# A fused attention kernel on one core: the second half of the first q on ScalarE, a K eviction in halves, and two half banks of the tail waited for one by one

## The chip, the cores and the metric

The kernel runs on one core of a Trainium2 chip. The metric is the device time of one execution in microseconds (us), taken as the median of several runs; less is better. The engines are named as in the profile: PE (TensorE: matmuls; PEld are its weight loads), DVE (VectorE), ACT (ScalarE), POOL (GpSimd) and SP (SyncE, which only issues DMAs here). ACTq and SPq are the DMA issues of ACT and SP.

## The reference

Two attention blocks read the same x (2048 tokens of 640), each with its own weights and 32 heads of 20: A is full softmax attention, B a sliding window of 8 keys, 2 apart. A gate of one number per token mixes them.

```python
    x = A_x
    g = _sigmoid((x * gate_w).sum(-1, keepdims=True))
    a = _A_ref(x, A_wqkv, A_wo)        # softmax(q k^T * scale) v, all 2048 keys, then @ wo
    b = _B_ref(x, B_wqkv, B_wo)        # the same over 8 keys at distances 0, 2, .. 14, then @ wo
    return g * a + (1 - g) * b
```

All inputs are bf16, and so is the output (2048 x 640).

## The kernel before

**Tiling.** The heads are taken four at a time ("quads", 8 of them), 32 partitions to a head, and the queries in chunks of 512, so there are 32 groups of (chunk, quad). A group has 64 units (16 blocks of 128 keys x 4 heads). A tile is two or three units: PE writes the scores of each into one PSUM bank of 512 columns (L1731), ACT takes the exponential of all of them in one instruction (L1756), and four units at a time PE multiplies them by v into the bank `obank` (L1801). Some units go to DVE instead of ACT, which makes powers of two by integer arithmetic (L1745, L905). Between the tiles PE, DVE and POOL do all the other work: projections of q, k and v, all of block B, and the output projections of earlier chunks (L632 is the line of their matmuls).

**What sets the order.** A planner (`_Sched`, and generators with priorities) runs at build time. It keeps a clock for each engine, an estimated duration for each task and, per buffer key, the last writer and the readers since. From the keys it derives the semaphore waits: a task waits for what last wrote the keys that it reads, and for the readers and the writer of those that it writes. `accum` adds to a key that another task has begun. What comes out is one fixed list of instructions for each engine. At the end of the start (from L1545 on) the planner's clocks and free times are overwritten by constants, so that what it plans after that follows from those constants.

**The start.** x is loaded, transposed by PE and copied to `xT`; the keys of the first quad are projected in four blocks of 512. The first three are evicted to `kT` by ACT (`k_out`, L1444), each behind a DVE instruction that finds the largest absolute value (L1437). The fourth is projected in two halves of 256 (L1497) into two banks of `score1`; DVE takes the maximum of each half (L1514), and ACT evicts both in one instruction (L1525). The first q is projected in two halves too, half 0 into `obank`, half 1 into the third bank of `score0`. A bound on the scores is subtracted inside the matmul: |q| of half 0 comes from ACT (L1517), of half 1 from DVE (L1522); the largest |k| (L1518) goes into the matrix `KM` (L1520); and PE adds KM x |q| to each half of q (L1531). Then DVE scales the two halves, adds an offset and writes them to `qT` as bf16 (L1535, twice). The first score tile (L1731) reads both halves. Behind L1535 DVE has the first v eviction (L1458), three instructions for constants (L554 to L557) and further v evictions (L833).

**The tail.** The last 512 tokens are four blocks of 128. Their output projection is nearly complete before the last group of heads is; `tail()` adds the last heads' part, with the matmuls at L1212. The columns 512 to 640 of all blocks lie in one bank ("strips", `score1`). The columns 0 to 512 of blocks 2 and 3 lie in two banks kept for them (`side0` and the third bank of `score0`, found in `tail_bank`), those of blocks 0 and 1 in the first two banks of `score0` ("halves"). DVE adds the earlier part to the strips (L1234), ACT evicts blocks 2 and 3 (L1240, twice), and DVE adds and evicts blocks 0 and 1 (L1243, twice). Then each block's 128 rows are stored by a DMA (L1248): blocks 2 and 3 issued by ACT, blocks 0 and 1 by SP. At the end SP waits for all DMAs, one semaphore after the other. The two halves share the buffer key `("score", 0)`, so both L1243 wait for whatever wrote that key last.

Of the kernel before, what the change touches and what calls it, by code (L numbers as in the profile page):

```python
# [10 lines left out]
ALU = mybir.AluOpType  # L11
ACTF = mybir.ActivationFunctionType
# [35 lines left out]
OCT = STEP * SCALE / LN2  # L48
# [324 lines left out]
def _ap(t, off, dims):  # L373

    row = 1
    for n in t.shape[1:]:
        row *= n
    return bass.AP(tensor=t, offset=off, ap=[[row, P]] + [list(d) for d in dims])


def _build(ctx, nc, A_x, A_wqkv, A_wo, B_wqkv, B_wo, gate_w, out):
# [3 lines left out]
    sch = _Sched(nc, ctx)  # L385
    T = sch.task
# [4 lines left out]
    score = [ps(1536, "score0"), ps(1536, "score1")]  # L391
# [4 lines left out]
    side = [t_[:, o_:o_ + 512] for t_, o_ in BANKS]  # L396
# [15 lines left out]
    kT = sb([P, NQ, S], BF16, "kT")  # L412
# [4 lines left out]
    qT = [sb([P, 512], BF16, "qT%d" % i) for i in range(NQF)] + [woBp[:, i, 0:512] for i in (2, 3)]  # L417
# [15 lines left out]
    offs = sb([P, 1], FP32, "offs")  # L433
# [7 lines left out]
    kmx4 = sb([P, 5], FP32, "kmx4")  # L441
# [5 lines left out]
    onesrow = sb([P, 1], FP32, "onesrow")  # L447
# [43 lines left out]
    dvc = lambda n, mode=1: 0.064 + n * 1.0417e-3 / mode  # L491
    actc = lambda n: 0.095 + n * 0.81e-3 if n > 512 else 0.0635 + n * 0.8334e-3
# [5 lines left out]
    def x_load(tcc, dur):  # L498
# [12 lines left out]
      writes=["WvA"], dma=True)  # L511
    T("sp", 12.0, lambda e: e.dma_start(_ap(kvw, WK_OFF, [[D, CN], [1, D]]), wA_v[:, :, D:2 * D]),
      writes=["WkA"], dma=True)
# [11 lines left out]
      reads=["rB"], writes=["ident"])  # L525
# [12 lines left out]
    for j in range(4):  # L538
        T("dve", 0.07, lambda e, j=j: e.memset(onesrow[32 * j:32 * j + 1, :], 1.0), writes=["onesrow"])
        T("dve", 0.1, lambda e, j=j: e.memset(KMmask[32 * j:32 * j + 32, 32 * j:32 * j + 1], -1.0078125),  # L540
          writes=["KMmask"])
    T("dve", 0.06, lambda e: e.tensor_copy(ones2[:, :], _ap(onesrow, 0, [[0, 2]])), reads=["onesrow"], writes=["ones2"])
    for i in range(NQF):
        T("pool", 0.4, lambda e, i=i: e.memset(qT[i][:, :].bitcast(FP32), 0.0), writes=[("qTz", i)])
    T("dve", 0.06, lambda e: e.tensor_scalar(offs[:, :], onesrow[:, :], STEP * TOP, None, op0=ALU.mult),
      reads=["onesrow"], writes=["offs"])
# [174 lines left out]
    qkeys = {}  # L721
# [410 lines left out]
    pre = lambda i: (dst2[:, 0:1024], qabs2[:, 0:1024], stage[:, 2048:3072])[i].bitcast(FP32)  # L1132
    tail_bank = {}

    def paired(of, blk):
        at = lambda j: blk * P + 2 * (j % 64) + j // 64
        return lambda j: of(slice(at(j), at(j) + 63, 2))
# [3 lines left out]
    def fold_mms(o, blk, qs, c0, c1, b_too, fs=range(CN)):  # L1141
        tok = slice(blk * P, (blk + 1) * P)
        if not b_too:
            return [(o, paired(lambda c: oN[1][:, c], blk), woA_l[:, c0:c1])]
        mms = [(o, oB[:, f, tok], woBp[:, f, c0:c1]) for f in range(CN)] if fs[0] == 0 else []
        wl = [woA_d[:, f, c0:c1] for f in range(CN - 1)] + [woA_z[:, c0:c1]]
        return mms + [(o, paired(lambda c, f=f: oTd[:, (QCN - 1) % 2, f, c], blk), wl[f]) for f in fs]
# [53 lines left out]
    def tail():  # L1201
        tout = [_ap(stage, 3 * 1024 + blk * D, [[1, D]]) for blk in range(4)]
        tcol = lambda blk, c0, c1: _ap(stage, 3 * 1024 + blk * D + c0, [[1, c1 - c0]])
        q = [NQ - 1]
        rd = ["oN1"] + WL

        def mm(key, lst, accum, rd=rd):
            def fn(e):
                seen = set()
                for o, l, r in lst:  # L1210
                    for j in range(0, P, 32):
                        ins = e.matmul(o[j:j + 32, :], l(j), r, start=not accum and o.offset // 512 not in seen, stop=True, skip_group_check=True)  # L1212
                    seen.add(o.offset // 512)
                return ins
            T("pe", sum(0.215 if o.shape[-1] > 128 else 0.06 for o, _, _ in lst), fn, reads=rd, mode="col",
              **({"accum": [key]} if accum else {"writes": [key]}))


        b3 = score[1]
        late = range(FE, CN)  # L1220
        rl = [("oTd", (QCN - 1) % 2, k) for k in range(NQ)] + ["woA_d"] + WQ
        strip = lambda blk: b3[:, blk * P:(blk + 1) * P]
        half = lambda blk: score[0][:, blk * 512:(blk + 1) * 512]
        first = lambda o, *a: [(o_, lambda j, l=l: l(slice(j, j + 32)) if not callable(l) else l(j), r) for o_, l, r in fold_mms(o, *a, True, late)]
        mm(("score", 1), [m_ for blk in range(4) for m_ in first(strip(blk), blk, q, 512, D)], False, rl)
        mm(("score", 0), [m_ for blk in range(2) for m_ in first(half(blk), blk, q, 0, 512)], False, rl)
        run_until(("norm", NG - 1))
        mm(("score", 1), [fold_mms(strip(blk), blk, q, 512, D, False)[0] for blk in range(4)], True)
        for blk in (2, 3):
            b = tail_bank[blk]  # L1230
            mm(("side", b), fold_mms(side[b][:, :], blk, q, 0, 512, False), True)
        for blk in range(2):
            mm(("score", 0), fold_mms(half(blk), blk, q, 0, 512, False), True)
        T("dve", dvc(512), lambda e: e.tensor_tensor(  # L1234
            _ap(stage, 3 * 1024 + 512, [[D, 4], [1, P]]), _ap(b3, 0, [[P, 4], [1, P]]),
            stage[:, 2048:3072].bitcast(FP32).rearrange("p (b c) -> p b c", c=P), ALU.add),
          reads=[("score", 1), ("pre", 2)], writes=["tout_r"])
        for blk in (2, 3):
            b = tail_bank[blk]
            T("act", actc(512), lambda e, b=b, blk=blk: e.activation(tcol(blk, 0, 512), side[b][:, :], ACTF.Copy),  # L1240
              reads=[("side", b)], writes=[("tout", blk)])
        for blk in range(2):
            T("dve", dvc(512), lambda e, blk=blk: e.tensor_tensor(  # L1243
                tcol(blk, 0, 512), score[0][:, blk * 512:(blk + 1) * 512], pre(blk), ALU.add),
              reads=[("score", 0), ("pre", blk)], writes=[("tout", blk)])
        for blk in (2, 3, 0, 1):
            row = (QCN - 1) * 512 + blk * P
            T("act" if blk > 1 else "sp", 2.0, lambda e, blk=blk, row=row: e.dma_start(out_v[row:row + P, :], tout[blk]),  # L1248
              reads=[("tout", blk), "tout_r"], writes=[("out", row)], dma=True)
# [131 lines left out]
    def run_until(flag, first=None):  # L1381
        n = 0
        while not done.get(flag):
            if not any(step(ent, 1e9, True) for ent in sorted(gens, key=lambda x: x[0] != first)):
                raise RuntimeError("stuck on %r: %r" % (flag, [e[3] for e in gens]))
            n += 1
# [114 lines left out]
    hcols = lambda h: slice(256 * h, 256 * h + 256)  # L1501
    k3 = lambda h: score[1][:, 512 * h:512 * h + 256]
    q0 = [obank[:, 0:256], side[1][:, 0:256]]
    q0k = ["obank", ("side", 1)]
    for h in range(2):
        T("pe", 0.55, half_proj(k3(h), lambda c: kvw[:, WKP_OFF + c * P:WKP_OFF + c * P + P], 1536 + 256 * h),
          reads=[("WkP", 0)] + XT(3), writes=[("K3", h), ("score", 1)])
    for h in range(2):
# [3 lines left out]
      reads=[("kmx4", i) for i in range(3)], writes=[("kmx", 0)])  # L1512
    for h in range(2):
        T("dve", dvc(256), lambda e, h=h: e.tensor_reduce(  # L1514
            kmx4[:, 3 + h:4 + h], k3(h), AX.X, ALU.max, apply_absolute_value=True),
          reads=[("K3", h)], writes=[("kmx4", 3 + h)])
    T("act", actc(256), lambda e: e.activation(qabs[0][:, 0:256], q0[0], ACTF.Abs), reads=[("Q0", 0)], writes=[("qabs", 0)])  # L1517
    T("dve", 0.1, lambda e: e.tensor_scalar(kmx[:, 0:1], kmx[:, 0:1], kmx4[:, 3:4], kmx4[:, 4:5], op0=ALU.max, op1=ALU.max),  # L1518
      reads=[("kmx", 0), ("kmx4", 3), ("kmx4", 4)], writes=[("kmx", 0)])
    T("dve", 0.2, lambda e: e.tensor_scalar(KM[0], KMmask, kmx[:, 0:1], None, op0=ALU.mult),  # L1520
      reads=[("kmx", 0), "KMmask"], writes=[("KM", 0)])
    T("dve", dvc(256), lambda e: e.tensor_scalar(  # L1522
        qabs[0][:, 256:512].bitcast(U16), q0[1].bitcast(U16)[:, 1:512:2], 0x7FFF, None, op0=ALU.bitwise_and),
      reads=[("Q0", 1)], writes=[("qabsh", 1)])
    t = T("act", actc(512), lambda e: e.activation(kT[:, 0, 1536:2048].rearrange("p (h c) -> p h c", c=256),  # L1525
                                               _ap(score[1], 0, [[512, 2], [1, 256]]), ACTF.Identity, bias=onesrow[:, 0:1]),
          reads=[("K3", 0), ("K3", 1), ("score", 1), "onesrow", ("kmx4", 3), ("kmx4", 4)], writes=[("kT", 0, 3)])
    bank_free[2] = t.end + LAT["act"]
    qah = [("qabs", 0), ("qabsh", 1)]
    for h in range(2):  # L1530
        T("pe", 0.11, lambda e, h=h: e.matmul(q0[h], KM[0], qabs[0][:, hcols(h)], start=False, stop=True, skip_group_check=True),  # L1531
          reads=[("KM", 0), qah[h]], accum=[("Q0", h), q0k[h]])
    v_first()
    for h in range(2):
        t = T("dve", dvc(256), lambda e, h=h: e.tensor_scalar(  # L1535
            qT[0][:, hcols(h)], q0[h], OCT, offs[:, 0:1], op0=ALU.mult, op1=ALU.add),
              reads=[("Q0", h), q0k[h], "offs", ("qTz", 0)], writes=[("qTh", h)])
        if h == 0:
            obank_first = t.end + LAT["dve"]
    bank_free[1] = t.end + LAT["dve"]  # L1540
# [1 line left out]
    v_out()  # L1542
    bank_free[0] = t.end + LAT["dve"] + 0.5
    done[("k", 0)] = done[("q", 0)] = True
    for key in qkeys[0]:  # L1545
        sch.bufs[key][0].end = 18.0655808
    sch.bufs["kT", 0, 3][0].end = 16.4994312
    sch.avail.update(pe=17.6032304, dve=18.2962528, act=16.4994312)
    bank_free[:] = [18.6485808, 16.6514312, 16.6514312]
# [359 lines left out]
    while pvg < NG:  # L1909
# [53 lines left out]
        elif pvg < NG:  # L1963
            run_side(sch.avail["pe"] + 1.0)
    run_until("prefold")
    tail()

    sch.emit()
# [28 lines left out]
```

## Time and profile before

| | |
|---|---|
| median of 3 runs | 790.83 us (790.8 to 791.33) |
| the profiled execution | 791.24 us, of which the span is 789.4 us |
| ACT busy | 769.0 us (97%), 732 instructions |
| PE busy | 752.3 us (95%), 12556 matmuls |
| DVE busy | 721.5 us (91%), 1282 instructions |
| POOL busy | 123.9 us (16%), 230 instructions |
| moved by DMA | 36.16 MB, 46 GB/s over the span |

A time in the timeline counts from the start of the span. A row gives the start, the time from the first to the end of the last instruction of the row, the engine, the line, the operation, the tiles written and read with their shapes, how many instructions it merges, and in brackets how long the engine had been idle and what released it. [...] A matmul's end is modelled.

### The profile page before, as it was taken

The numbers are of one execution on the slowest core, as the hardware profiler recorded it, in microseconds if no ns is written. First come the engines' busy times: TensorE is split into PE (matmuls) and PEld (weight loads), VectorE is DVE, ScalarE is ACT, GpSimd is POOL, SyncE is SP. The second block draws the span as 40 slices with busy tenths as digits, with TensorE's granted clock in tenths as the row PEclk, the third lists the DMA queues.
The fourth block names the chain that finished last, engine by engine and source line by source line (L and its number), as shares of the span: only waits on it lengthen the run. The fifth ranks groups of instructions, "written<-read, shape, count | busy, mean of one in ns | idle before, by whom it ended". The sixth has DMA issues, their size and how long they took to land.

```text
span 789.4 us, 29584 instructions
## 1 busy us (share of the span) xinstructions
PE 752.3 (95%) x12556; PEld 290.6 (37%) x12556; DVE 721.5 (91%) x1282; ACT 769.0 (97%) x732; POOL 123.9 (16%) x230
## 2 busy tenths in 40 slices
PE   8999999999999999999999999999999999999997
PEld 5423333232233334333334433434443433344323
DVE  7798888999999989999988999998999999898894
ACT  4999999999999999999999999999999999999996
POOL 4011202111112011111111101111111111111210
PEclk9999999999999999999999999999999999999999
DMA  7241121010021123130111312012113013100311
GB/s 227 62 109 25 40 44 33 14 24 18 8 71 30 41 42 73 24 72 16 23 40 42 76 41 58 14 41 71 25 31 71 26 24 71 46 7 7 74 31 40
DMA packets 62663, 36.16 MB, mean 46 GB/s; under 512 B 26884, under 2 KB 61972, under 8 KB 62532
## 3 DMA queue, kind: packets, MB, share of 16 engines
q1 hardware_dynamic: 62244, 33.94, 17.9%
q8 instruction: 100, 1.64, 0.9%
q10 hardware_dynamic: 288, 0.33, 0.1%
q14 instruction: 31, 0.25, 0.1%
HBM read 12.85 MB, written 3.54 MB: 21 GB/s over the span
## 4 chain that ended last, share of the span: by engine, by line
PE 43%; ACT 26%; DVE 17%; issue 11%; SPq 2%; DMA 1%; POOL 0%; DVEq 0%; ACTq 0%
ACT ebuf L1756 25%; PE score L1731 13%; PE obank L1801 12%; PE side L632 12%; DVE uD L1745 6%; DVE eD L905 4%; PE score L632 2%; DVE kvw L1092 1%; SPq L975 1%; DVE qkvB L967 1%; DMA oTd<-in_A_x_dram 1%; PE obank L1822 1%; PE score L1822 1%; PE side L1003 1%; DVE kvw L993 1%
## 5 line engine op out<-in xcount | busy, mean ns | idle before, releaser
L1756 ACT ACTIVATE ebuf<-score 128x1024 bf16<-128x1024 f32 (+1 forms) x699 | 757.0, 1266 | 4.4 <-PE score L1731 3.7
L1745 DVE TENSOR_SCALAR uD<-score 128x512 int16<-128x512 f32 x392 | 260.2, 680 | 14.7 <-PE score L1731 13.3
L1731 PE MATMUL score<-qT,kT 32*128 32x512 bf16 x1856 | 253.8, 384 | 17.7 <-ACT ebuf L1756 13.6
L905 DVE TENSOR_SCALAR eD<-uD 128x2048 int16<-128x2048 int16 x294 | 195.0, 687 | 4.5 <-PE obank L1801 3.4
L1801 PE MATMUL obank<-ebuf,vA 128*21 128x512 bf16 x1656 | 153.5, 385 | 1.7 <-DVE oTt L865 0.6
L1731 PEld LDWEIGHTS score<-qT,kT 32*128 32x128 bf16 x1856 | 63.0, 91 | 211.6 <-ACT ebuf L1756 147.4
L925 POOL TENSOR_TENSOR vS<-vA,vw 128x252 bf16<-128x252 bf16 x98 | 59.9, 613 | 388.5 <-DVE eD L905 252.8
L1801 PE MATMUL obank<-eD,vS 128*21 128x512 bf16 x1176 | 103.5, 379 | 0.0
L632 PE MATMUL side<-xT,wBs 128*32 128x256 bf16 x2400 | 93.6, 280 | 2.2 <-DVE oB L1125 0.7
L632 PEld LDWEIGHTS side<-xT,wBs 128*32 128x32 bf16 x2400 | 68.1, 141 | 27.9 <-issue 14.5
L1801 PEld LDWEIGHTS obank<-ebuf,vA 128*21 128x21 bf16 x1656 | 36.0, 89 | 83.0 <-issue 56.4
L1092 DVE TENSOR_TENSOR kvw<-kvw,eB 128x2048 bf16<-128x2048 bf16 x40 | 48.1, 1214 | 0.2 <-DMA kvw<-qkvB 0.2
L993 DVE TENSOR_TENSOR kvw<-qkvB 128x2048 bf16<-128x2048 bf16 x40 | 48.0, 1215 | 0.1
L882 POOL TENSOR_TENSOR oN<-oTt,rcp 128x256 bf16<-128x256 f32 x62 | 38.8, 625 | 58.0 <-DVE eD L905 39.5
L967 DVE CAST qkvB<-side 128x512 bf16<-128x512 f32 (+1 forms) x72 | 42.0, 593 | 4.5 <-PE side L632 4.3
L873 POOL TENSOR_TENSOR rcp<-rcp,gA 128x16 f32<-128x16 f32 x31 | 9.1, 292 | 192.0 <-DVE eD L905 90.9
L1801 PE MATMUL obank<-uD,vA 128*21 128x512 bf16 x392 | 38.1, 379 | 0.0
L1801 PEld LDWEIGHTS obank<-eD,vS 128*21 128x21 bf16 x1176 | 28.8, 91 | 19.8 <-issue 2.0
L1731 PE MATMUL score<-woBp,kT 32*128 32x512 bf16 x192 | 30.0, 384 | 1.8 <-ACT ebuf L1756 1.6
L632 PE MATMUL side<-xT,kvw 128*32 128x512 bf16 (+1 forms) x360 | 30.1, 382 | 0.6 <-DVE vA L833 0.3
L632 PE MATMUL side<-kvw,xT 128*32 128x160 bf16 (+1 forms) x740 | 28.5, 263 | 1.3 <-DVE vA L833 0.5
L865 DVE STREAM_TRANSPOSE oTt<-obank 128x512 f32<-128x512 f32 x32 | 22.6, 707 | 6.5 <-PE obank L1801 6.5
(194 smaller groups left out, 555.8 us busy)
## 6 DMA issues: line engine op xcount, KB each, us to landing
kvw<-qkvB SPq DMA_DIRECT2D x128, 80.6 KB
wBs<-in_B_wqkv_dram SPq DMA_DIRECT2D x15, 160.0 KB
WqP<-in_A_wqkv_dram SPq DMA_DIRECT2D x14, 160.0 KB
oTd<-oN SPq DMA_DIRECT2D x108, 20.0 KB
out_dram<-outsb SPq DMA_DIRECT2D x12, 160.0 KB
qT<-dst SPq DMA_DIRECT2D x93, 20.0 KB
kvw<-in_A_wqkv_dram SPq DMA_DIRECT2D x2, 800.0 KB
oTd<-in_A_x_dram SPq DMA_DIRECT2D x2, 640.0 KB
```

Of the source, the lines that this page charges most:

```text
L632: ins = e.matmul(o[j:k, :], l(j) if callable(l) else l[:, j:k], r, start=(first and i == 0), stop=(last and i == n - 1), skip_group_check= ...
L865: T("dve", 0.625, lambda e: e.transpose(oTt[:, :], obank[:, :]), reads=["obank"], writes=["oTt"])
L882: T(en, c2 if n == 4 else 0.56, lambda e, oo=oo, ii=ii, ib=ib: e.tensor_tensor(oo, ii, ib, ALU.mult), reads=["rcp", "oTt"], **{"accum" if ...
L905: T("dve", 0.065 + 0.1334 * n, lambda e, k=k, sl=sl: e.tensor_scalar(eD[:, sl % NS, 0:512 * n].bitcast(I16), uD[d % 2][:, 0:512 * n].bitca ...
L925: T("pool", 0.607, lambda e: e.tensor_tensor(vS[:, d % 2, :, :], _ap(vA, (kb * NQ + q) * 4 * DV, [[0, K - 1], [1, 4 * DV]]), _ap(vw, 0, [[ ...
L967: t = TB(dvc(n * TOK), lambda e, o=o, i=i: e.tensor_copy(o, i), reads=[("side", b)], writes=[key])
L993: TB(dvc(CH, 2), lambda e: e.tensor_tensor(o, i0, i1, ALU.mult), reads=["qB", "kB"], writes=[("prod", i)] + (["WkA", "WvA", ("WkP", 0)] if ...
L1092: TB(dvc(CH, 2), lambda e: e.tensor_tensor(o, i0, i1, ALU.mult), reads=["eB"] + [("vR", w4) for w4 in range(4)], writes=[("prod", i)], por ...
L1731: ins = e.matmul(o, kT[32 * j:32 * j + 32, q, kb * P:(kb + 1) * P], qT[qbuf[g]][32 * j:32 * j + 32, :], start=True, stop=True)
L1745: t = T("dve", 0.598, lambda e: e.tensor_scalar(uD[d % 2][:, 512 * i:512 * (i + 1)].bitcast(I16), side[x], UOFF, 0.0, op0=ALU.add, op1=ALU ...
L1756: exps[s] = T("act", actc(512 * n), lambda e: e.activation(ebuf[s % NE][:, 0:512 * n], score[s % 2][:, 0:512 * n], ACTF.Exp, scale=LN2 / S ...
L1801: ins = e.matmul(obank[32 * j:32 * j + DV, :], v, src, start=(kb == 0), stop=(last and k >= len(lst) - 4), skip_group_check=True)
```

## The change

Four edits.

1. The eviction of the fourth block of keys (L1525, ACT, 512 columns) becomes two of 256 columns. Each waits for the maximum of its own half; the first stands ahead of L1517 on ACT, the second right behind it.
2. Half 1 of the first q is written to `qT` by ACT and not by DVE. Half 0 stays on DVE. The first score tile so waits for both engines.
3. In the tail the four last matmul groups change their order from block 2, block 3, half 0, half 1 to block 2, half 0, block 3, half 1. The halves get buffer keys of their own, `("hb", 0)` and `("hb", 1)`, and each L1243 waits for its own.
4. The planner's constant for the end of the second q half becomes 17.8; the other constants stay.

```diff
-              **({"accum": [key]} if accum else {"writes": [key]}))
+              **({"accum": [key]} if accum else {"writes": [key] if key[0] != "score" or key[1] else [key, ("hb", 0), ("hb", 1)]}))
...
-        for blk in (2, 3):
-            b = tail_bank[blk]
-            mm(("side", b), fold_mms(side[b][:, :], blk, q, 0, 512, False), True)
-        for blk in range(2):
-            mm(("score", 0), fold_mms(half(blk), blk, q, 0, 512, False), True)
+        for h in range(2):
+            b = tail_bank[2 + h]
+            mm(("side", b), fold_mms(side[b][:, :], 2 + h, q, 0, 512, False), True)
+            mm(("hb", h), fold_mms(half(h), h, q, 0, 512, False), True)
...
-              reads=[("score", 0), ("pre", blk)], writes=[("tout", blk)])
+              reads=[("hb", blk), ("pre", blk)], writes=[("tout", blk)])
...
+    def k3_out(h):
+        return T("act", actc(256), lambda e: e.activation(
+            kT[:, 0, 1536 + 256 * h:1792 + 256 * h], k3(h), ACTF.Identity, bias=onesrow[:, 0:1]),
+          reads=[("K3", h), ("score", 1), "onesrow", ("kmx4", 3 + h)], **{"accum" if h else "writes": [("kT", 0, 3)]})
+
+    k3_out(0)
     T("act", actc(256), lambda e: e.activation(qabs[0][:, 0:256], q0[0], ACTF.Abs), reads=[("Q0", 0)], writes=[("qabs", 0)])
+    t = k3_out(1)
...
-    t = T("act", actc(512), lambda e: e.activation(kT[:, 0, 1536:2048].rearrange("p (h c) -> p h c", c=256),
-                                               _ap(score[1], 0, [[512, 2], [1, 256]]), ACTF.Identity, bias=onesrow[:, 0:1]),
-          reads=[("K3", 0), ("K3", 1), ("score", 1), "onesrow", ("kmx4", 3), ("kmx4", 4)], writes=[("kT", 0, 3)])
...
-        t = T("dve", dvc(256), lambda e, h=h: e.tensor_scalar(
-            qT[0][:, hcols(h)], q0[h], OCT, offs[:, 0:1], op0=ALU.mult, op1=ALU.add),
-              reads=[("Q0", h), q0k[h], "offs", ("qTz", 0)], writes=[("qTh", h)])
+        if h == 0:
+            fn = lambda e: e.tensor_scalar(qT[0][:, hcols(0)], q0[0], OCT, offs[:, 0:1], op0=ALU.mult, op1=ALU.add)
+        else:
+            fn = lambda e: e.activation(qT[0][:, hcols(1)], q0[1], ACTF.Identity, scale=OCT, bias=offs[:, 0:1])
+        t = T(("dve", "act")[h], dvc(256), fn, reads=[("Q0", h), q0k[h], "offs", ("qTz", 0)], writes=[("qTh", h)])
...
-    for key in qkeys[0]:
-        sch.bufs[key][0].end = 18.0655808
+    sch.bufs["qTh", 0][0].end = 18.0655808
+    sch.bufs["qTh", 1][0].end = 17.8
```

## The prediction

> **What bounds the kernel now.** I read the page first, then the timeline of the two places that the change touches (14.8 to 19 us and 784 to 789 us), then the DMA share of the last stretch. The page's busy times and its chain, by engine:
>
> ```profile
> PE 752.3 (95%) x12556; PEld 290.6 (37%) x12556; DVE 721.5 (91%) x1282; ACT 769.0 (97%) x732; POOL 123.9 (16%) x230
> ...
> PE 43%; ACT 26%; DVE 17%; issue 11%; SPq 2%; DMA 1%; POOL 0%; DVEq 0%; ACTq 0%
> ```
>
> ACT, PE and DVE are all above 90% and the chain hands over between them, so the middle has no single bound. The listings of both programs, with what each row waits for, are equal on all five engines between the first score tile and the last four matmul groups: the change pins the planner's clocks to almost the old values behind the start. So the middle can only shift as a whole, and two ends are left to work out.
>
> **The start.** The first score tile (L1731) needs both halves of the first q.
>
> ```profile
> start us, us, engine line op out<-in xcount [idle before <-releaser]
> ...
> 15.89 0.38 ACT L1517 ACTIVATE qabs<-obank 128x256 bf16<-128x256 f32 x1 [0.45 <-PE obank L1497]
> ...
> 16.17 0.68 ACT L1525 ACTIVATE kT<-score,onesrow 128x512 bf16<-128x512 f32 x1
> ...
> 16.92 0.28 PE L1531 MATMUL score<-qabs,eB 128*128 128x256 bf16 x1
> ...
> 17.24 0.48 DVE L1535 TENSOR_SCALAR qT<-score,offs 128x256 bf16<-128x256 f32 x1
> ...
> 17.78 0.39 PE L1731 MATMUL score<-qT,kT 32*128 32x512 bf16 x3 [0.23 <-DVE qT L1535]
> ...
> 18.10 0.53 PE L632 MATMUL score<-kvw,xT 128*32 128x160 bf16 x20
> ...
> 18.69 0.33 DVE L833 CAST vA<-score 128x160 bf16<-128x160 f32 x1
> ```
>
> See that the second DVE write of qT starts at 17.24, 0.04 behind the end of its matmul (16.92 + 0.28 = 17.20). DVE's first half does not hold it up, so a second engine cannot start it earlier. After: ACT starts at 17.20 + 0.05 = 17.25 (0.05 is ACT behind PE in the tail rows below: 784.17 + 0.39 to 784.61). Its duration is on no row, since no ACT row is Identity with a pointer bias on 256 columns. From below it is the 0.38 of L1517, which has no pointer; from above the 0.68 of L1525, which is twice as wide. I take 0.47: L1517's 0.38 plus 0.09, which is L1525's 0.68 less the 0.60 of a 512-wide ACT copy without a pointer (L1240). That ends at 17.72, just where DVE ended (17.24 + 0.48), and PE follows 0.05 to 0.06 later, at 17.78 as before: **0.00**. The ends are -0.09 and +0.21. [...]
>
> DVE is rid of 0.48. L1458, at 17.64 in the timeline, then waits for its own matmuls (17.04 + 0.51 = 17.55) and starts at 17.60, 0.04 earlier, as do the constants behind it. But L833 at 18.69 waits for L632's end (18.10 + 0.53 = 18.63), behind the unmoved score tile: the 0.04 are given back there.
>
> The K eviction in halves costs ACT 2 x 0.47 for 0.68. The first half needs the first maximum (L1514, on DVE to 15.25) and ACT, whose previous eviction (14.76 + 0.69) lets the next begin some 0.10 before its end, as L1525 does behind L1517: 15.35 to 15.82. Queued behind it is L1517, whose matmul holds it until 15.89 anyway, with 0.17 to spare. If that cover were gone, KM x |q| on PE would wait with it. The second half takes 16.17 to 16.64, and ACT is free for the q half at 17.25. PE's added wait names DVE first (half 0, done at 17.31) and ACT second, so what is queued behind it waits for nothing new. No DMA, SP or POOL row moves: **0**.
>
> **The tail.** Four groups of four matmuls end it: block 2, block 3, half 0, half 1. They become block 2, half 0, block 3, half 1, and DVE's first add waits for half 0 alone. The columns are as above.
>
> ```profile
> 784.17 0.39 PE L1212 MATMUL side<-outsb,oN 128*32 128x512 bf16 x4
> ...
> 784.39 0.82 PE L1212 MATMUL score<-outsb,oN 128*32 128x512 bf16 x12
> 784.40 0.69 DVE L1234 TENSOR_TENSOR kvw<-score,kvw 128x512 bf16<-128x512 f32 x1 [0.54 <-PE score L1212]
> 784.61 0.60 ACT L1240 ACTIVATE kvw<-side 128x512 bf16<-128x512 f32 x1 [3.76 <-PE side L1212]
> 785.11 0.59 ACT L1240 ACTIVATE kvw<-score 128x512 bf16<-128x512 f32 x1
> 785.24 0.85 ACTq L1248 DMA_DIRECT2D out_dram<-kvw  x2
> 785.26 0.69 DVE L1243 TENSOR_TENSOR kvw<-score,dst 128x512 bf16<-128x512 f32 x1 [0.17 <-PE score L1212]
> 785.87 0.68 DVE L1243 TENSOR_TENSOR kvw<-score,qabs 128x512 bf16<-128x512 f32 x1
> 785.98 0.96 SPq L1248 DMA_DIRECT2D out_dram<-kvw  x2
> ```
>
> The three groups at 784.39 end 0.22 apart, at 784.77, 784.99 and 785.21; DVE's first L1243 starts 0.05 behind the last. Two adds follow each other in 0.61 (785.26 to 785.87), so behind L1234 the first can start at 784.40 + 0.61 = 785.01, with half 0 ready at 784.77. The second starts at 785.62, behind half 1 at 785.21: its new wait is already met. Both adds, and SP's two DMAs queued on them, come **0.25 earlier**. Block 3 now ends at 784.99; ACT could take it at 785.04 but is busy until 785.11, so ACT's two DMAs stay (0.07 to spare).
>
> Does 0.25 reach the end? The DMA share, by stretch:
>
> ```profile
> core 0: us, PE busy (x) PEld busy (x) DVE busy (x) ACT busy (x) POOL busy (x), PEclk, DMA share, GB/s
> 786.10:786.60 0.50, 0.00 (x0) 0.00 (x0) 0.45 (x1) 0.00 (x0) 0.00 (x0) 1.00 0.90 315
> 786.60:787.05 0.45, 0.00 (x0) 0.00 (x0) 0.00 (x0) 0.00 (x0) 0.00 (x0) 1.00 0.98 344
> 787.05:787.50 0.45, 0.00 (x0) 0.00 (x0) 0.00 (x0) 0.00 (x0) 0.00 (x0) 1.00 1.03 361
> 787.50:788.10 0.60, 0.00 (x0) 0.00 (x0) 0.00 (x0) 0.00 (x0) 0.00 (x0) 1.00 0.83 301
> ```
>
> Last but one column: the 16 engines are busy from the first packet to the last. The four stores (0.66 MB, 0.45 us each) run end to end, ACT's two from 786.1 to 787.05, then SP's two. ACT's first store sets when this begins, and it does not move; what SP issues earlier stands in line. Only the idle share inside can be filled, at most 0.10 x 0.50 + 0.02 x 0.45 = 0.06, and part of that is the ramp at the start. I take **-0.03**. Bounds: -0.25, if all passes through, and +0.15, which is block 3's 0.22 less 0.07 if ACT's slack does not cover it. [...] The trace's last packet lands at 788.14, and SP goes on at 788.49 through its row of waits, which does not change.
>
> **The sum.** 0.00 + 0 - 0.03 = -0.03. The profiled execution took 791.24 (789.4 of span and 1.8 around it) and would take 791.21. It lies 0.41 above the median of the runs, 790.83; my time is that median less 0.03: **790.80**.
>
> **The rivals.**
> - *The tail's 0.25 reach the end*: 790.83 - 0.25 = 790.58. For it: the chain of waits ends on these adds and not on a DMA. Against it: the four rows above. This would need the last 0.45 us of stores to start without queueing. [...] Chance 0.18.
> - *Slower: the wait on DVE becomes a longer one on ACT.* Place: between L1531's end and the first score tile. It decides from an ACT write of 0.475 us on; at L1525's full 0.68 the price is 0.21, which nothing takes back, since the tile, L632 and L833 move with it: 791.04. For it: L1444's and L1525's 0.68 to 0.69 are the only rows of this form. Against it: ACT's rows grow with width (0.38 to 0.60 for 256 to 512 columns). Chance 0.14.
> - *The middle falls into another phase*: equal order, but ACT, PE and DVE meet otherwise. The three runs spread over 0.53; to matter it must be three times that. Both signs, 0.05 each: 789.2 or 792.5.
> - *The change doesn't do what it says*: ruled out by the listing, where the second add has a PE wait of its own and the q half stands on ACT. It would leave 790.83, which is the forecast's time.
>
> **Numbers.** Forecast 0.58, rivals 0.18, 0.14, 0.10. The bounds add up to -0.34 (790.49) and +0.36 (791.19); with the runs' scatter, which goes upward from 790.80 to 791.33, I give 790.4 to 791.4. It holds the first three cases. 0.2% is 1.6 us, about what a measurement of this kernel can tell from no change; only the phase case passes it, so faster 0.05, same 0.90, slower 0.05.
>
> **What would show it.** Start: the ACT write of q at 17.25 for 0.47, the first score tile at 17.78, L833 at 18.69; a tile after 17.85 speaks for the slower rival. Tail: adds at 785.01 and 785.62, SP's DMAs near 785.73 and 786.33, ACT's unmoved, the last packet near 788.1 counted from the same point; a last packet at 787.9 proves the first rival. I am wrong if the stretch between the first tile and the last exponential changes its length by more than 0.5 us.

## The result and the profile after

The changed kernel takes **792.34 us** (median of 22 runs, 791.7 to 797.77), beside 790.71 us for the kernel before in the same session (22 runs, 790.35 to 791.49). The ratio is 1.0021, with a 95% interval of 1.0014 to 1.0029: slower by 1.63 us, between 1.1 and 2.3. I had forecast 790.80 and a range that ends at 791.4.

The profiled execution after takes 792.42 us, 790.3 of it span. Of the 1.18 us between the two profiled executions 0.88 lie inside the span. The time around the span (2.1 us, beside 1.8 before) goes from 1.75 to 2.2 in the executions of either kernel, so the loss is to be looked for inside. The page after, its first lines and the chain by engine:

```profile
span 790.3 us, 29589 instructions
...
PE 752.9 (95%) x12556; PEld 291.5 (37%) x12556; DVE 720.8 (91%) x1281; ACT 769.8 (97%) x734; POOL 123.9 (16%) x230
...
PE 42%; ACT 27%; DVE 17%; issue 11%; SPq 1%; DMA 0%; POOL 0%; ACTq 0%; DVEq 0%
```

The busy times barely move: DVE loses 0.7 us for one instruction less, ACT gains 0.8 for two more. No share of the chain names a new bound. The page has no row that explains 1.6 us, so I measured four stretches between the same events in both traces.

| stretch | before, us | after, us |
|---|---|---|
| end of KM x \|q\| of half 1 (L1531 before) to the first score tile | 0.580 | 0.655 |
| second exponential to last exponential | 759.62 | 759.18 |
| start of the strips' add (L1234 before) to the semaphore of the last store, as SP's wait on it is met | 4.093 | 5.178 |
| from there to the end of the span | 0.956 | 0.956 |

The start is 0.08 longer and the end 1.09 longer; the middle is not longer at all. First the start, in the timeline after:

```profile
16.88 0.48 DVE L1539 TENSOR_SCALAR qT<-obank,offs 128x256 bf16<-128x256 f32 x1
...
17.29 0.47 ACT L1541 ACTIVATE qT<-score,offs 128x256 bf16<-128x256 f32 x1 [0.60 <-PE score L1534]
...
17.88 0.12 PEld L1736 LDWEIGHTS score<-qT,kT 32*128 32x128 bf16 x3 [0.48 <-DVE qT L1539]
...
17.91 0.39 PE L1736 MATMUL score<-qT,kT 32*128 32x512 bf16 x3 [0.31 <-ACT qT L1541]
...
18.82 0.33 DVE L833 CAST vA<-score 128x160 bf16<-128x160 f32 x1
```

ACT's write takes the 0.47 that I gave it and ends at 17.77. But the tile comes at 17.91, 0.14 behind it. The brackets tell why. The weight load ahead of the matmul names DVE as its releaser, although DVE's half was done long before ACT's: the load carries the wait for DVE itself, and the late one, for ACT, is a wait instruction of its own ahead of it (17.81 to 17.86 in the trace's records).

Now the tail, in the timeline after:

```profile
784.19 0.69 DVE L1233 TENSOR_TENSOR kvw<-score,kvw 128x512 bf16<-128x512 f32 x1 [0.55 <-PE score L1212]
784.80 0.68 DVE L1242 TENSOR_TENSOR kvw<-score,dst 128x512 bf16<-128x512 f32 x1
785.03 0.86 ACTq L1247 DMA_DIRECT2D out_dram<-kvw  x2
785.40 0.68 DVE L1242 TENSOR_TENSOR kvw<-score,qabs 128x512 bf16<-128x512 f32 x1
785.51 0.96 SPq L1247 DMA_DIRECT2D out_dram<-kvw  x2
```

The two adds follow the strips' add by 0.61 and 1.21 us (0.86 and 1.47 before; an add takes 0.69, and the next starts 0.08 before its end): they come the 0.25 earlier that the edit was to give. SP issues its stores 1.32 behind the strips' add, beside 1.58 before. And yet the last store is done 1.09 later. The DMA share by stretch, with columns as in the table of the prediction:

```profile
785.90:786.40 0.50, 0.00 (x0) 0.00 (x0) 0.18 (x1) 0.00 (x0) 0.00 (x0) 1.00 0.91 310
786.40:786.90 0.50, 0.00 (x0) 0.00 (x0) 0.00 (x0) 0.00 (x0) 0.00 (x0) 1.00 1.03 358
786.90:787.40 0.50, 0.00 (x0) 0.00 (x0) 0.00 (x0) 0.00 (x0) 0.00 (x0) 1.00 0.98 353
787.40:788.00 0.60, 0.00 (x0) 0.00 (x0) 0.00 (x0) 0.00 (x0) 0.00 (x0) 1.00 0.69 239
788.00:788.40 0.40, 0.00 (x0) 0.00 (x0) 0.00 (x0) 0.00 (x0) 0.00 (x0) 1.00 0.06 24
```

To 788.0 this is much the picture of before: the engines are full (0.91 to 1.03 until 787.4), and the stores queue. The last row is new: a share of 0.06, as much as one engine of 16 would give, goes on for 0.4 us. What it carries stands in the queue view of 787.9 to 788.4 of the trace after (queue and kind, packets, MB, share of the 16 engines):

```profile
q14 instruction: 1, 0.01, 3.9%
q1 hardware_dynamic: 5, 0.00, 2.3%
```

One packet of 8 KB of a kind that no line of the kernel issues: *instruction*. It starts at 788.00 and takes 0.31 us; five small store packets lie in the same stretch, and the last two end at 788.37, 0.36 behind all the others. In the trace before, the same view of the whole stretch of the stores, 786 to 789.5, has only the stores:

```profile
q10 hardware_dynamic: 288, 0.33, 27.0%
q1 hardware_dynamic: 288, 0.33, 26.1%
```

There the instruction packet went out at 783.85, before any of the stores. The view of 783.7 to 784.4 before:

```profile
q8 instruction: 1, 0.02, 11.4%
q14 instruction: 1, 0.01, 4.1%
```

Queue 8 is of the same kind, with packets of 16 KB; its last one lies ahead of all stores in every trace here (0.26 us ahead of the strips' add before, 0.19 after), so it can't make the difference. Last, the waits of SP in the last 8 us (line waited for: us in total, times, longest), first before, then after:

```profile
SPq L351 <- DMA out_dram<-kvw: 1.4, 2, 1.0
```

```profile
SPq L351 <- DMA out_dram<-kvw: 2.8, 2, 1.7
```

SP waits 1.4 us longer for the stores, of which about 0.26 is only that it begins to wait earlier. The semaphore of the last store comes 1.00 us behind its last packet, and not 0.355 as before. So the 1.09 are 0.44 of data that ends later (4.18 instead of 3.74 behind the strips' add) and 0.65 of a later semaphore.

### The profile page after: what moved, and what is told of

It is laid out like the page before. It is cut to its first block, busy times and chain, and to the rows that moved or that the text cites. A ratio compares the mean times of both kernels' runs of the same rounds, so it can differ in the third digit from the quotient of the medians.

```text
span 790.3 us, 29589 instructions
## 1 busy us (share of the span) xinstructions
PE 752.9 (95%) x12556; PEld 291.5 (37%) x12556; DVE 720.8 (91%) x1281; ACT 769.8 (97%) x734; POOL 123.9 (16%) x230
## 3 DMA queue, kind: packets, MB, share of 16 engines
q8 instruction: 100, 1.64, 0.9%
## 4 chain that ended last, share of the span: by engine, by line
PE 42%; ACT 27%; DVE 17%; issue 11%; SPq 1%; DMA 0%; POOL 0%; ACTq 0%; DVEq 0%
ACT ebuf L1761 26%; PE score L1736 12%; PE obank L1806 12%; PE side L632 11%; DVE uD L1750 6%; DVE eD L905 4%; PE score L632 2%; SPq L975 1%; DVE qkvB L967 1%; DVE kvw L1092 1%; PE side L1003 1%; DVE vA L833 1%; PE score L1827 1%; PE obank L1827 1%; PE score L1399 1%
```

## The theories

- **F**, the instruction packet: DVE has one instruction fewer in the program (1472 records in the trace instead of 1473, with its waits), so the 8 KB packet goes out at another point and falls among the last stores. It alone costs the 1.09 us at the end; the tail edit has no part in it.
- **T**, the tail: SP's stores, issued earlier, collide with ACT's, and the last one ends later for that.
- **S**, the start: what comes later at the start is the loss, or shifts what follows.
- **N**: there is no cause, and executions scatter in that way.

In the experiments "the end" is the third row of the table above, and "the packet" is the instruction packet of queue 14 next to the tail. Times of runs are medians; the ratio to the kernel before on the same chip, given with its interval, is not exactly that of the two medians. Each kernel has one traced execution. In these three later sessions the kernel before gave 791.64, 791.11 and 791.41, with single runs up to 796 (the changed kernel's up to 797); its scatter makes the intervals wider than in the first, so the verdicts rest mainly on the segments of the profiled executions.

## The experiments

**The edits one by one.** The first kernel has all of the change but the tail edit; the second has the tail edit alone.

```diff
# e1: as after, without
-        mm(("hb", h), fold_mms(half(h), h, q, 0, 512, False), True)
...
-              reads=[("hb", blk), ("pre", blk)], writes=[("tout", blk)])
# e2: as before, with
+        mm(("hb", h), fold_mms(half(h), h, q, 0, 512, False), True)
...
+              reads=[("hb", blk), ("pre", blk)], writes=[("tout", blk)])
```

> The kernel before with the start's edits alone (K eviction in halves, second q half on ACT); the tail as before. Theory F (instruction packet): the start's edits take one instruction out of DVE's stream, so the last 8 KB packet of the instruction queue goes at about 788 us instead of 783.8, among the last stores, and the last store's semaphore comes about 1 us after its data instead of 0.36: then this kernel is as slow as the changed one, 1.2 to 1.7 us above before, and the packet lies behind 786. Theory T (the tail): the new order of the stores makes the last semaphore late: then this kernel is within 0.3 us of before and the packet, wherever it lies, does no harm. Theory S (the start): the first score tile comes 0.1 later and the middle falls into a slower phase: 1.2 to 1.7 above before, with a tail that is as long as before.

Measured: 792.29 us, ratio 1.0005 (0.9986 to 1.0023). First tile 0.655, end 5.040, packet 3.68 us behind the strips' add. The loss is there without the tail edit.

> The kernel before with the tail's edit alone (four groups in the new order, the half banks waited for one by one). DVE has as many instructions as before. Theory F: the packet lies near 783.8 as before, and the time is within 0.15 us of before, since the stores queue on the DMA engines; the strips' add to the last data packet takes 3.7 to 3.8 us in both. Theory T: 1.2 to 1.7 us above before. Theory S: as theory F. If the 0.25 us of the earlier adds reach the end, 0.25 below before.

Measured: 791.14 us, ratio 0.9998 (0.9986 to 1.001). First tile 0.580, end 4.091 (4.093 before), packet 0.55 us ahead of the strips' add, as before. SP's wait in this trace:

```profile
SPq L351 <- DMA out_dram<-kvw: 1.7, 2, 1.1
```

0.3 longer than before, since SP begins to wait 0.26 earlier, and done at the same time. T falls: in the trace the end with the tail edit alone is neither shorter nor longer.

**DVE's instruction count, on the changed kernel.** Eight small DVE memsets of an unused tile, 32 bytes to a partition, at the place of the constant `offs` in the start:

```diff
+    pad = sb([P, 8], FP32, "pad")
...
-    T("dve", 0.06, lambda e: e.tensor_scalar(offs[:, :], onesrow[:, :], STEP * TOP, None, op0=ALU.mult),
+    T("dve", 0.06, lambda e: [e.memset(pad[:, i:i + 1], 0.0) for i in range(8)] and e.tensor_scalar(offs[:, :], onesrow[:, :], STEP * TOP, None, op0=ALU.mult),
```

> The changed kernel with eight tiny DVE memsets ahead of L545, where DVE idles for 1.1 us; nothing else. Theory F: DVE's stream crosses the border seven instructions earlier than in the kernel before, the packet goes at or before 783.8, and the time comes down to within 0.3 us of before. Theories T and S: as slow as the changed kernel, 1.2 to 1.7 us above before.

Measured: 791.25 us, ratio 0.9999 (0.999 to 1.0009). First tile 0.656 as after, end 4.086. The packet went out 16.4 us ahead of the strips' add. The changed kernel with eight instructions *more* has the old end.

**The count, on the kernel before.** One DVE memset fewer and nothing else: two small constant tiles become one, so that one memset fills both.

```diff
-    zero = sb([P, 32], BF16, "zero")
...
-    onesrow = sb([P, 1], FP32, "onesrow")
+    onez = sb([P, 17], FP32, "onez")
+    onesrow, zero = onez[:, 0:1], onez[:, 1:17].bitcast(BF16)
...
-    T("dve", 0.1, lambda e: e.memset(zero[:, :], 0.0), writes=["zero"])
...
-    T("dve", 0.06, lambda e: e.memset(onesrow[:, :], 0.0), writes=["onesrow"])
+    T("dve", 0.06, lambda e: e.memset(onez[:, :], 0.0), writes=["onesrow", "zero"])
...
```

> The kernel before, in which one DVE memset of the start is saved by putting two constants into one tile; start and tail as before. Theory F: DVE's stream is one instruction shorter, as in the changed kernel; the packet moves to about 788 and the time to 1.2 to 1.7 us above before. Theories T and S: no change (within 0.2 us).

Measured: 791.77 us, ratio 1.0 (0.9986 to 1.0014). First tile 0.580, end 5.141, packet 3.78 us behind the strips' add. The queue view of 785.8 to 789.4 and SP's wait in this trace:

```profile
q10 hardware_dynamic: 288, 0.33, 26.3%
q1 hardware_dynamic: 288, 0.33, 25.6%
q14 instruction: 1, 0.01, 0.5%
```

```profile
SPq L351 <- DMA out_dram<-kvw: 2.5, 2, 1.4
```

The old kernel has the new end, with none of the four edits, as soon as DVE's program is one instruction shorter. Its start is that of before, so S falls as a cause of the loss at the end. This trace speaks most plainly for F; the whole time does not (the median is 0.13 above its session's, where 1.2 to 1.7 were expected).

**The changed kernel again, and with one instruction put back.** The first is the changed kernel with no edit, to be compared on the same chip; the second has one memset of `pad` instead of eight, so that DVE's count is that of before while ACT keeps its five more (1448 records in the trace instead of 1443).

> The changed kernel once more, beside the others of this call. Theory F (an 8 KB instruction packet among the last stores): packet near 788, last semaphore 5.0 to 5.2 us behind the strips' add, time 1.1 to 1.6 us above before. Theory N (the first measurement was scatter): within 0.3 us of before.

Measured: 792.49 us (791.82 to 797.1), ratio 1.0009 (0.9991 to 1.0027). First tile 0.656, end 5.177, packet 3.81 behind the strips' add: the profiled execution of the result, repeated. N falls for the end.

> The changed kernel with one tiny DVE memset ahead of L545, so that DVE has as many instructions as in the kernel before. Theory F: the packet goes 0.5 us ahead of the strips' add as in the kernel before (near 783.8), the last semaphore comes 4.1 us behind that add, and the time is 0.0 to 0.2 us above before, of which 0.08 is the later first score tile. Theory N, or a cause elsewhere in the changed kernel: the same as the changed kernel in this call.

Measured: 791.4 us (790.46 to 795.12), ratio 0.9996 (0.998 to 1.0012). First tile 0.656, end 4.089, packet 0.55 ahead. One memset in the start, hundreds of us before, takes the loss at the end away. The medians of the two differ by 1.09 and the lowest times by 1.36. ACT's five more instructions do nothing to the end.

**The order of the two waits.** As the last kernel, and in the code that writes out PE's waits ACT's half of q is sorted to the front, so that the weight load itself carries it:

```diff
-                        for d in sorted(t.deps, key=lambda x: -x.end - lat(x, sname)):
+                        for d in sorted(t.deps, key=lambda x: -99.0 if x.idx in self.first and sname == "pe" else -x.end - lat(x, sname)):
...
+    sch.first.add(sch.bufs["qTh", 1][0].idx)
```

> As the last one, and the first score tile's wait on DVE stands ahead of that on ACT, so that the late one is the instruction's own. From the end of KM x |q| of half 1 to the first tile: 0.58 us as in the kernel before, where the changed kernel takes 0.655; if the wait's place is not the cause, 0.655 stays. Theory F for the rest: time within 0.15 us of before; with the tail's earlier adds worth 0.25, as much below.

Measured: 790.78 us (790.27 to 797.46), ratio 0.9992 (0.9971 to 1.0012). First tile 0.567, beside 0.655 with the waits as in the change and 0.580 before. End 4.085. In its timeline:

```profile
17.38 0.47 ACT L1543 ACTIVATE qT<-score,offs 128x256 bf16<-128x256 f32 x1 [0.60 <-PE score L1536]
...
17.91 0.39 PE L1739 MATMUL score<-qT,kT 32*128 32x512 bf16 x3 [0.22 <-ACT qT L1543]
```

ACT's write ends at 17.85 and the tile starts 0.06 behind it, not 0.14: the 0.08 of the start are the order of two waits, and ACT's write itself is no slower than DVE's. As a whole it can't be told from the kernel before.

**A control: the kernel before with eight memsets more.**

> The kernel before with the eight tiny DVE memsets. Theory F: the packet goes some 16 us earlier, where no store is under way, and the time stays within 0.15 us of before. If eight memsets or a packet elsewhere cost something by themselves, 0.3 us or more above before.

Measured: 791.77 us (790.58 to 795.39), ratio 1.0002 (0.9985 to 1.0019). First tile 0.581, end 4.104; the packet went out 16.5 us ahead of the strips' add. The median lies 0.66 above its session's, further than I expected, but the interval holds both, and the segments show no place for it: start and end are as before, and the middle of the profiled execution is 760.11, inside the 758.6 to 761.2 that all these kernels span. As a whole time it is inconclusive; its end agrees with F.

**SP's last waits.** On the kernel before, SP's final waits are put in the order in which the DMAs were issued, so that the last store is waited for last.

```diff
+                        last = {t.sem: t.idx for l in self.lists.values() for t in l if t.dom == "dma"}
-                        for sem, tot in self.dma_final.items():
+                        for sem, tot in sorted(self.dma_final.items(), key=lambda x: last[x[0]]):
```

> The kernel before, in which SP's waits at the end stand in the order in which the DMAs were issued, so that the last store's semaphore is waited for last and not third of twelve. In every trace so far the end of the span comes 0.956 us behind that semaphore, nine waits of 0.061 each among it. If those waits are on the path, the end comes 0.40 to 0.46 behind it and the time is 0.5 us below before; if they are not, 0.956 stays. The instruction packet near 783.8 should not move, as SP's stream keeps its length.

Measured: **790.46 us** (789.73 to 792.1, 12 runs) beside 791.41, ratio 0.9986 (0.9972 to 0.9999). From the last store's semaphore to the end of the span 0.468, not 0.956. SP's wait for the stores:

```profile
SPq L352 <- DMA out_dram<-kvw: 0.8, 2, 0.4
```

Eight waits that are long met stood behind the last store's, one each 0.061 us in the trace: 8 x 0.061 = 0.488, which is what the segment lost. They now pass while the stores are still on their way. The 0.49 are shown by the segment; the medians differ by 0.95, which is more than it explains. This kernel is the only one whose interval lies below the kernel before, if by a hair (0.9999), and it leaves the change out.

**Where the tail's 0.25 went.** Two kernels, the one before and the one with the tail edit alone, in which ACT's two last stores write 32 columns in place of 640, so that most of blocks 2 and 3 of the last 512 tokens is left out of the output.

```diff
-            T("act" if blk > 1 else "sp", 2.0, lambda e, blk=blk, row=row: e.dma_start(out_v[row:row + P, :], tout[blk]),
+            T("act" if blk > 1 else "sp", 2.0, lambda e, blk=blk, row=row: e.dma_start(out_v[row:row + P, 0:32] if blk > 1 else out_v[row:row + P, :], tcol(blk, 0, 32) if blk > 1 else tout[blk]),
```

> The kernel before, with ACT's two stores cut to 32 of 640 columns (the rest of blocks 2 and 3 is left out of the output), so that nothing stands ahead of SP's stores on the DMA engines. Only the stretch from the strips' add to the last store's semaphore is of interest, beside the next kernel: 3.7 to 4.1 us here.

> The tail's edit alone, with ACT's two stores cut to 32 of 640 columns in the same way (the rest of blocks 2 and 3 is left out of the output). If the tail's 0.25 us is lost because the stores queue on the DMA engines, it shows here: the stretch from the strips' add to the last store's semaphore is 0.22 to 0.28 shorter than in the kernel with the old tail and the same cut. If it is lost elsewhere (the issue on SP, the receipt of the last store), both stretches are equal within 0.05.

Measured, one run each: end 4.014 without the tail edit and 3.743 with it; the last data packets are at 3.653 and 3.380 behind the strips' add. With ACT's stores out of the way the edit gains 0.27; with them, 0.00 (4.091 beside 4.093). The 0.25 are lost on DMA engines that the stores keep busy, as the four rows of the DMA share said (0.83 to 1.03).

The segments of all kernels but these two, worked out from the records of the traces (us; the packet is counted from the start of the strips' add):

| kernel | first tile | middle | end | packet |
|---|---|---|---|---|
| before | 0.580 | 759.62 | 4.093 | -0.55 |
| after | 0.655 | 759.18 | 5.178 | +3.81 |
| e1, no tail edit | 0.655 | 760.03 | 5.040 | +3.68 |
| e2, tail edit alone | 0.580 | 758.61 | 4.091 | -0.55 |
| e3, after, DVE +8 | 0.656 | 761.18 | 4.086 | -16.4 |
| e4, before, DVE -1 | 0.580 | 759.45 | 5.141 | +3.78 |
| e5, after again | 0.656 | 758.74 | 5.177 | +3.81 |
| e6, after, DVE +1 | 0.656 | 759.04 | 4.089 | -0.55 |
| e7, e6 and the waits' order | 0.567 | 759.09 | 4.085 | -0.55 |
| e8, before, DVE +8 | 0.581 | 760.11 | 4.104 | -16.5 |
| e9, before, SP's waits | 0.580 | 759.08 | 4.100 | -0.54 |

The end has two values, 4.09 to 4.10 and 5.04 to 5.18, and the column beside it says which: it is long in exactly the four traces in which the packet lies among the stores. In these four it follows the packet closely: the last store's semaphore comes 1.363 to 1.366 us behind the start of the packet, although the packet's place varies by 0.14. It does not follow the data: in e1 the last data packet ends latest of the four (4.183) and the semaphore comes earliest (5.040). The whole times sort in the same way by their lowest runs: 791.5 to 791.8 for those four, 790.6 and below for all others. The medians do not show it as clearly, and most missed what was expected of them: beside their sessions' kernel before e1 lies 0.65 above (1.2 to 1.7 expected) and e4 0.13 (1.2 to 1.7), e2 0.50 below (within 0.15), e3 0.39 below (within 0.3), e6 0.29 above (0.0 to 0.2), e7 0.33 below (within 0.15, or 0.25 below); e5 alone came as expected, 1.38 above. All these intervals hold 1, so as whole times they decide nothing.

## Why the prediction was wrong

**The step that failed** is the sentence "No DMA, SP or POOL row moves: 0". A DMA did move, one that no engine of the kernel issues: the instruction packet, from 0.55 us ahead of the strips' add to 3.81 behind it. I counted every instruction that the change moves on an engine and every queue of SP and ACT, and not that a q half taken off DVE makes DVE's program one shorter (1472 records for 1473), with which the packet's place changes, nor that such packets move on the DMA engines beside the stores. The page before has shown the packets all along, in its third part: two queues of kind *instruction*, 14 (31 packets, 0.25 MB) and 8 (100, 1.64 MB), beside the two of the kernel's own. With it failed "SP goes on at 788.49 through its row of waits, which does not change". The row of waits is the same (0.956 in both), but what it waits for came 1.09 later. This term I had at 0 without a bound, so the range could not hold it.

**The start, +0.08 where I had 0.00.** The cost of ACT's write was right (0.47 forecast, 0.473 measured). What failed is "PE's added wait names DVE first (half 0, done at 17.31) and ACT second, so what is queued behind it waits for nothing new". PE meets them the other way round. The code sorts the waits by planned end, with the latest planned first, and in the traces of after and e7 the first in that order rides on the instruction itself. ACT's wait is the separate one because edit 4 pins ACT's end to 17.8, and DVE's stays at 18.07. In the trace the separate wait ends at 17.856 and the load starts at 17.882; e7 swaps the two and the 0.655 become 0.567. The slower rival thus had the right place with the wrong mechanism: not a longer ACT write, and 0.08 instead of 0.21. As that rival had said, L833 moves with the tile: it comes 0.08 later than forecast, counted from the same matmul.

**The tail, right.** The adds came 0.25 earlier, as worked out; the gain at the end was 0.00 where I had -0.03, and e10 and e11 show the reason that I gave, full DMA engines. One reading in it was off, that what SP issues earlier "stands in line": with the edit (e2) SP's first store packet goes out 2.20 us behind the strips' add and not 2.66, and ACT's last one ends at 3.29 and not 2.83. The stores share the engines, and the last packet ends at 3.74 in both. The first rival (790.58) falls with e2. What was split here is a wait: the adds did complete sooner (by 0.25), and the end came no sooner while the stores queued behind them (0.00), and 0.27 sooner when ACT's stores were out of the way.

**The K halves and the middle, right as far as they can be seen.** The two halves take 0.47 each on ACT, at 15.40 and 16.23, and |q| of half 0 between them is not delayed: it starts at 15.95 (15.89 before), in a trace that lies 0.05 to 0.06 later from 13.9 us on. The order of the middle is unchanged, and its length varies between 758.6 and 761.2 from trace to trace with no relation to the edits: before 759.62, after 759.18 and 758.74.

**The sum.** 1.085 + 0.075 = 1.16 us are shown in the segments, inside the interval of 1.1 to 2.3 of the measured loss. That the start's 0.08 reach the end is not shown, since the middle varies by more than that. What may lie between 1.16 and the median's 1.63 is not settled either; a later pair on one chip, e5 and e6, differs by 1.09 in its medians and by 1.36 in its lowest times.

**What stays open.** That DVE's count decides when the packet goes out is shown in both directions, by e3, e4 and e6, for instructions of the start. Which instruction sets it off is not: one instruction fewer moved it 4.4 us later, and seven more than before (e3) or eight (e8) moved it 16 us earlier, and I did not find a row that it follows. That the packet shares a DMA engine with the late store packets I conclude from their times, and from the share of 0.06 after 788.0. That the semaphore keeps 1.36 us behind the packet's start the four traces show; why it needs so long, 1.02 to 1.06 behind the packet's end where before it needs 0.355 behind the data, no run shows. The traces show that the semaphore follows the packet and not the data, but which engine carried what they don't tell. The "border" in what was expected of e3 was a guess of mine: no run shows one.

## What to carry to other kernels

Where the time ends in stores, look at the instruction packets too: one instruction more or less, hundreds of us earlier, can put one of them among the last stores (here a DVE instruction of the start, and 1.1 us). A kernel that is "slower" by this much need not have been slowed by what its edit is about: before blaming that, compare the packet's place, and restore the instruction count with a harmless memset. Where two waits meet on one instruction, the one that comes last belongs on the instruction itself (0.08 here), and where one engine collects all DMAs at the end, the last store's wait belongs last (0.49 here).

## What the runs showed that I had not expected

- The chain of waits does not show this loss. In both traces it ends on DVE's end marker, just behind the last add, with a DMA share of 0 or 1%; the 1.09 us lie in a tail that the chain leaves out. The DMA share by stretch and SP's waits show it.
- A single 8 KB packet of 0.31 us went with a loss of 1.09, in two parts: the last store data ended 0.44 later than before, and the semaphore came another 0.65 later behind them.
- A wait that was already met took SP 0.061 us, in the traces of before and after. Eight of them at the very end were 0.49 us, more than any of the four edits was worth.
